# Where the product of gate and value is done, who makes the low parts of the gate weights, and the order of the second stage

## The chip, the cores and the metric

The kernel runs on one core of a Trainium2 chip. The metric is the time of one execution in microseconds (us). Five engines work side by side, each with its own list of instructions that it takes in order: PE (TensorE, matrix products), DVE (VectorE), ACT (ScalarE), POOL (GpSimd) and SP (SyncE, which here only issues DMA transfers). PEld is PE's loading of weights.

## The reference

A linear recurrence with complex decay over 768 steps (4 batches, 8 heads, 48 values per head) gives 3072 tokens of 384 values. Two feed-forward layers follow:

```python
for t in range(S):
    new_re = ar * S_re - ai * S_im
    new_im = ar * S_im + ai * S_re
    S_re, S_im = (new_re + kv, new_im)
    y[:, :, t] = np.einsum('bhd,bhde->bhe', q[:, :, t], S_re)
...
xn = x / rms * rms_g
g = xn @ w_gate                       # 384 x 1536
silu = g * (1.0 / (1.0 + np.exp(-g)))
val = xn @ w_val
x = silu * val @ w_out                # 1536 x 384
...
h = x @ w_in                          # 384 x 2048
g = h * np.clip(h + 3.0, 0.0, 6.0) / 6.0
return g @ w_out                      # 2048 x 384
```

## The kernel before

**Precision.** Each matrix product of the two layers is made in PE's rounded fp32 type as three products: every factor is split into a high part (a copy in the rounded type) and a low part (the value less its high part), and `mm3` (L743 to 746) adds high by high, high by low and low by high.

**First stage.** The recurrence is cut into seven units of 32 or 64 steps (L444 to 455 are the scan's pairs of `m` and `P` on DVE; `Sst`, `X`, `T` and `LAt` are tiles of the scan, the decay and the state). `flip` (L714 to 728) ends a part of a unit: it writes 256 tokens as `xh` (ACT) and `xl` (DVE, L728). Then `steps_M` (L748) does the first product for these tokens: 12 columns of blocks j, gate and value, three parts k, three products each of 256 columns, written to a PSUM tile `pm` that two j share; there are two such tiles. One tile takes 36 products. For each, `silu` (L761) has ACT write the silu of the gate half to `sg` (L765; two tiles), DVE multiply it by the value half in PSUM (L767), and SP store it to `u_dr` in DRAM (L769). There are 72 of these, 66 of them while the scan still runs.

**The gate weights.** They come as 12 pieces of raw 64-bit words, loaded by L320. `split_weights` (L325) turns one into high and low part `wg`: DVE decodes it in three steps (L304, 306, 308) into the single tile `wdA`, ACT checks its range (L315, 316, Abs and Sign), scales by the norm's weights (L335, three instructions) and writes the high part (L336), and DVE subtracts (L363, in a helper that sends some of its calls to POOL). The tile `wdA` is free for the next piece after that.

**The order.** All of the first stage up to the last unit is issued by `emit` (L853): a string, `ORDER`, names the step whose next part is issued, for the five engines together, and the set `ON_POOL` names the steps whose helper calls go to POOL. No scheduler moves anything there. What stands late in an engine's list waits for what is ahead of it.

**Second stage.** Blocks of 512 tokens. `steps_out1` (L900) fetches `uu` from `u_dr`, three tiles ahead (L907), splits it (`uh` on ACT, L913; `ul` on DVE, L914), multiplies by `wo` into `po`, and evicts the result as `x2b`. `steps_moe2` (L942) multiplies by `wi` into `ph`, applies the gate (ACT L957, 959, DVE L958, 960), multiplies by `w2` and stores the output. The first blocks are issued by L995 and L1003 with a fixed order of DVE and POOL, the rest by a loop at the end that the scheduler orders. In between stands a check of flags (L1007 to 1027), for which DVE waits for a small transfer.

Of the kernel before, what the change touches and what calls it, by code (L numbers as in the profile page):

```python
# [26 lines left out]
BLK = 512  # L27
KZ = 0.4995
# [205 lines left out]
def attn_moe(tc, io, dbg=None):  # L234
    nc = tc.nc
# [6 lines left out]
    u_dr = dram.tile([J1, 128, NT], F32, name="u_dr")  # L242

# [3 lines left out]
    gcol = const.tile([128, KT], F32, name="gcol")  # L247
    flags = const.tile([128, 11 * NU], F32, name="flags")
# [17 lines left out]
    nc.vector.memset(biasz[:, 5:6], -TINY_BELOW)  # L266
    SGN, MA, MB, NEGHALF, EPS = (cst[:, i:i + 1] for i in range(5))
# [57 lines left out]
    def split_weights(j):  # L325
        raw = wraw.pop(j)
        A = wdA
        yield from to_f32(raw, 768, A)
        range_check(raw, 768, j, 'act')
        yield  # L330
        wg[j] = wA.tile([128, 2, KT, 2, 128], F32R, name="wg", tag=f"w{j}")
        hi, lo = wgv(j)
        A = A.bitcast(F32).rearrange("p (k w n) -> p k w n", k=KT, w=2)
        for k in range(KT):
            nc.scalar.activation(A[:, k], A[:, k], AF.Copy, scale=gcol[:, k:k + 1])  # L335
        nc.scalar.activation(hi, A, AF.Copy)  # L336
        yield
        ttx(lo, A, hi.bitcast(F32), ALU.subtract)
# [409 lines left out]
    def steps_M(u, st, h):  # L748
# [371 lines left out]
```

## Time and profile before

| | us |
|---|---|
| median of 3 runs (lowest, highest) | 1209.68 (1208.75, 1217.75) |
| profiled execution | 1209.66 |
| its span | 1207.5 |
| busy: PE, PEld | 1073.3 (89%), 930.2 (77%) |
| busy: DVE, ACT, POOL | 780.2 (65%), 561.9 (47%), 114.4 (9%) |

The span is the profiled execution from its first to its last instruction. Busy shares over the span are averages over stages that differ: up to about 110 us the weights are decoded and the scan begins, up to about 612 us scan and first product run together, up to about 640 us the last unit's product runs, and the rest is the second stage. PE's busy time is not its useful share at full speed, since products overlap in their pipeline.

### The profile page before, as it was taken

Reading aid. Unit: us, or ns where it says so; the run is one execution under the profiler, and the core shown is the slowest. Engines: PE = TensorE matmul, PEld = TensorE weight load, DVE = VectorE, ACT = ScalarE, POOL = GpSimd, SP = SyncE. Lnnn points to the kernel's source line nnn. Section 1 sums busy time; section 2 is a strip of 40 time slices with the busy share of each in tenths; the row PEclk is TensorE's granted clock in tenths of the full one; section 3 lists DMA queues with packets and bytes.
Section 4 is the critical chain, followed back from the end, with each engine's and each line's share of the span. In section 5 each row is a group of like instructions: output and inputs, shape, how many; then the busy total and the mean of one; then the engine's idle time right before and its main releaser. Section 6 shows DMA issues by size and latency. Waiting matters only on the chain.

```text
span 1207.5 us, 24626 instructions
## 1 busy us (share of the span) xinstructions
PE 1073.3 (89%) x10264; PEld 930.2 (77%) x10264; DVE 780.2 (65%) x1483; ACT 561.9 (47%) x922; POOL 114.4 (9%) x124
## 2 busy tenths in 40 slices
PE   0175699998999998999999999899999999999997
PEld 0165588888898888888988888688888888888885
DVE  4989989899788897788878788243333333333332
ACT  5568576575656754552333444243333333333332
POOL 3010010011012003011022212000000000000000
PEclk9999799999999999999989999899999999999999
DMA  8323545635535625627356544210220220100000
GB/s 333 132 51 85 162 92 155 176 98 182 146 93 166 161 73 185 170 52 218 112 177 208 175 132 75 56 37 1 70 62 1 62 69 1 61 27 1 27 1 29
DMA packets 77977, 124.27 MB, mean 103 GB/s; under 512 B 31841, under 2 KB 50402, under 8 KB 77218
## 3 DMA queue, kind: packets, MB, share of 16 engines
q1 hardware_dynamic: 77858, 122.63, 34.9%
q8 instruction: 82, 1.34, 0.5%
q14 instruction: 37, 0.30, 0.1%
HBM read 80.33 MB, written 34.60 MB: 95 GB/s over the span
## 4 chain that ended last, share of the span: by engine, by line
PE 55%; DVE 6%; DMA 3%; ACT 1%; issue 1%; SPq 0%; DVEq 0%; ACTq 0%
PE po L745 9%; PE po L746 9%; PE po L744 9%; PE ph L744 5%; PE ph L745 5%; PE ph L746 5%; PE pm L744 3%; PE pm L745 3%; PE pm L746 3%; PE psT L606 1%; DVE m L451 1%; DMA ok_dr<-okc 1%; DVE P L455 1%; PE psY L696 1%; DMA V<-in_v_dram 1%
## 5 line engine op out<-in xcount | busy, mean ns | idle before, releaser
L744 PE MATMUL pm<-xh,wg 128*128 128x256 f32 x864 | 256.7, 297 | 30.0 <-ACT sg L765 20.6
L745 PE MATMUL pm<-xl,wg 128*128 128x256 f32 x864 | 244.6, 283 | 2.5 <-DVE xl L728 2.5
L746 PE MATMUL pm<-xh,wg 128*128 128x256 f32 x864 | 243.9, 282 | 0.0
L744 PEld LDWEIGHTS pm<-xh,wg 128*128 128x128 f32 x864 | 165.7, 192 | 41.8 <-ACT sg L765 26.0
L745 PEld LDWEIGHTS pm<-xl,wg 128*128 128x128 f32 x864 | 166.0, 192 | 3.5 <-DVE xl L728 3.5
L746 PEld LDWEIGHTS pm<-xh,wg 128*128 128x128 f32 x864 | 165.9, 192 | 0.0
L958 DVE SCALAR_TENSOR_TENSOR r<-r,ph 128x512 f32<-128x512 f32 x96 | 65.8, 685 | 106.3 <-ACT r L957 106.3
L960 DVE TENSOR_TENSOR gl<-r,gh 128x512 fp32r<-128x512 f32 x96 | 68.0, 708 | 94.6 <-ACT gh L959 94.1
L957 ACT ACTIVATE r<-ph,biasz 128x512 f32<-128x512 f32 x96 | 65.8, 687 | 117.3 <-PE ph L746 117.2
L745 PE MATMUL po<-gl,w_h 128*128 128x512 f32 x288 | 114.7, 398 | 3.8 <-DVE gl L960 3.8
L746 PE MATMUL po<-gh,w_l 128*128 128x512 f32 x288 | 114.5, 398 | 0.0
L744 PE MATMUL po<-gh,w_h 128*128 128x512 f32 x288 | 114.1, 396 | 0.0
L746 PE MATMUL ph<-x2b,wi_l 128*128 128x512 f32 x288 | 113.7, 395 | 0.0
L745 PE MATMUL ph<-x2b,wi_h 128*128 128x512 f32 x288 | 113.7, 395 | 0.0
L744 PE MATMUL ph<-x2b,wi_h 128*128 128x512 f32 x288 | 113.6, 396 | 0.0
L959 ACT ACTIVATE gh<-r 128x512 fp32r<-128x512 f32 x96 | 60.6, 632 | 107.3 <-PE po L746 83.4
L914 DVE TENSOR_TENSOR ul<-uu,uh 128x512 fp32r<-128x512 f32 x72 | 51.8, 721 | 75.5 <-ACT uh L913 75.4
L913 ACT ACTIVATE uh<-uu 128x512 fp32r<-128x512 f32 x72 | 45.3, 630 | 91.3 <-PE po L746 84.3
L745 PE MATMUL po<-ul,wo 128*128 128x512 f32 x216 | 85.1, 394 | 0.6 <-DVE ul L914 0.6
L744 PE MATMUL po<-uh,wo 128*128 128x512 f32 x216 | 85.0, 394 | 0.0
L746 PE MATMUL po<-uh,wo 128*128 128x512 f32 x216 | 84.7, 392 | 0.0
L765 ACT ACTIVATE sg<-pm 128x512 f32<-128x512 f32 x72 | 42.6, 597 | 76.4 <-PE pm L746 70.7
(143 smaller groups left out, 2013.0 us busy)
## 6 DMA issues: line engine op xcount, KB each, us to landing
u_dr<-sg SPq DMA_DIRECT2D x72, 256.0 KB, 3.0
uu<-u_dr SPq DMA_DIRECT2D x72, 256.0 KB, 2.7
raw<-in_wo_dram SPq DMA_DIRECT2D x28, 384.0 KB, 3.7
wraw<-in_wgv_dram SPq DMA_DIRECT2D x12, 768.0 KB, 13.8
S<-in_s_all_dram SPq DMA_DIRECT2D x24, 384.0 KB, 3.7
K<-k_dr SPq DMA_DIRECT2D x40, 224.0 KB, 4.4
LAt<-in_a_all_dram SPq DMA_DIRECT2D x5, 1536.0 KB, 6.8
JS<-Sst SPq DMA_DIRECT2D x52, 144.0 KB, 4.0
```

The source lines that it names most:

```text
L451: tt(out=m4, in0=la, in1=pj, op=ALU.mult)
L455: tt(out=pn, in0=m4[:, :, 0], in1=m4[:, :, 1], op=ALU.add)
L744: nc.tensor.matmul(ps, lhsT=wh, rhs=xh, start=first, stop=False)
L745: nc.tensor.matmul(ps, lhsT=wh, rhs=xl, start=False, stop=False)
L746: nc.tensor.matmul(ps, lhsT=wl, rhs=xh, start=False, stop=last)
L765: nc.scalar.activation(sg, pm[:, :, 0], AF.Silu)
L913: nc.scalar.activation(uh, uu, AF.Copy)
L914: (nc.gpsimd if n < 0 else nc.vector).tensor_tensor(out=ul, in0=uu, in1=uh.bitcast(F32), op=ALU.subtract)
L957: nc.scalar.activation(r, ph, AF.Relu, bias=biasz[:, 2:3], scale=sixth)
L958: stt(out=r, in0=r, scalar=1.0, in1=ph, op0=ALU.min, op1=ALU.mult)
L959: nc.scalar.activation(gh, r, AF.Copy)
L960: tt(out=gl, in0=r, in1=gh.bitcast(F32), op=ALU.subtract)
```

## The change

1. The second stage takes the blocks of tokens in the order 4, 5, 0, 1, 2, 3.
2. For the tokens of blocks 0 to 3 (two thirds), `silu` no longer multiplies. ACT writes the silu to `sg`, and copies the value half from PSUM to `va`; both are stored, to `u_dr` and to a new `v_dr`. `sg` and `va` share three tiles. The second stage fetches both (`uu`, `vv`) and DVE multiplies them there, ahead of the split. 48 of the 72 products move; 24 stay where they were.
3. The low part of a gate weight is made by PE: ACT scales by the negated norm weights (so `wdA` holds the negative), writes the high part with scale -1, PE adds the two by fp32 products with the identity into a PSUM tile `pw` (of the same two tiles as `pm`), and ACT evicts it with scale -1. DVE's 12 subtractions go.
4. `ORDER` and `ON_POOL` are new; the latter has 20 entries in place of 25. ACT loads its tables 37 times in place of 43.

```diff
+BLOCKS = [4, 5, 0, 1, 2, 3]
...
-    "0F1f003b7zgjbXkH000G0H0I0J0K0L120M0N0O0R0P0Q0R0R01020R0R0R020S0S0S030S03040S05060908070b0S0a0b0c0c0d0d0e0e0f0f0T0T0T0T0g0g0h0h0i0T0i0k0k0l0l0m0m0T0j0U0U0U0U0j0n"
+    "0F1f7zgj00kH3bbX000G0H0I0K0L0M120J0N0O0R0P0Q0R0R0R010R020R020S0S0S0R030S030S04050S0809060T070a0T0S0T0b0b0T0c0c0d0d0T0e0e0f0T0f0g0g0h0h0i0i0k0j0k0U0T0l0U0l0U0U0m"
...
-ON_POOL = {124, 258, 285, 376, 549, 551, 561, 656, 779, 799, 808, 827, 829, 831, 841, 936, 1103, 1107, 1109, 1111, 1113, 1125, 1356, 1360, 1372}
+ON_POOL = {2, 19, 258, 267, 493, 771, 799, 818, 819, 821, 845, 936, 1059, 1088, 1098, 1101, 1103, 1331, 1353, 1362}
...
+    v_dr = dram.tile([J1, 128, NT], F32, name="v_dr")
...
+    ngcol = const.tile([128, KT], F32, name="ngcol")
...
+    nc.vector.tensor_scalar(out=ngcol, in0=gcol, scalar1=-1.0, scalar2=None, op0=ALU.mult)
...
         for k in range(KT):
-            nc.scalar.activation(A[:, k], A[:, k], AF.Copy, scale=gcol[:, k:k + 1])
-        nc.scalar.activation(hi, A, AF.Copy)
+            nc.scalar.activation(A[:, k], A[:, k], AF.Copy, scale=ngcol[:, k:k + 1])
+        nc.scalar.activation(hi, A, AF.Copy, scale=-1.0)
         yield
-        ttx(lo, A, hi.bitcast(F32), ALU.subtract)
+
+        pw = psM.tile([128, 2, 2, 256], F32, name="pw", tag="m", bufs=2)
+        for o, n in ((0, 2), (2, 1)):
+            pwo = pw[:, o // 2].rearrange("p a n -> p (a n)")[:, 0:n * 256]
+            for i, x in enumerate((A, hi.bitcast(F32))):
+                nc.tensor.matmul(pwo, lhsT=ident, rhs=x[:, o:o + n].rearrange("p k w n -> p (k w n)"), start=i == 0, stop=i == 1)
+        yield
+        nc.scalar.activation(lo.rearrange("p k w n -> p (k w n)"), pw.rearrange("p a b n -> p (a b n)")[:, 0:768], AF.Copy, scale=-1.0)
...
-            sg = mo.tile([128, 2, 256], F32, name="sg", tag="sg")
+            sg = mo.tile([128, 2, 256], F32, name="sg", tag="sg", bufs=3)
             table(None)
             nc.scalar.activation(sg, pm[:, :, 0], AF.Silu)
             yield
+            if t0 // BLK not in BLOCKS[:2]:
+                va = mo.tile([128, 2, 256], F32, name="va", tag="sg", bufs=3)
+                nc.scalar.activation(va, pm[:, :, 1], AF.Copy)
+                yield
+                nc.sync.dma_start(u_dr[j - 1:j + 1, :, t0:t0 + 256].rearrange("j p t -> p j t"), sg)
+                nc.sync.dma_start(v_dr[j - 1:j + 1, :, t0:t0 + 256].rearrange("j p t -> p j t"), va)
+                return
             tt(out=sg, in0=sg, in1=pm[:, :, 1], op=ALU.mult)
...
+        cols = slice(BLOCKS[n] * BLK, (BLOCKS[n] + 1) * BLK)
...
-            nc.sync.dma_start(uu, u_dr[j, :, n * BLK:(n + 1) * BLK])
+            nc.sync.dma_start(uu, u_dr[j, :, cols])
+            if n >= 2:
+                hold["v", j] = mu.tile([128, BLK], F32, name="vv", tag="vv", bufs=3)
+                nc.sync.dma_start(hold["v", j], v_dr[j, :, cols])
...
+            if n >= 2:
+                tt(out=uu, in0=uu, in1=hold.pop(("v", j)), op=ALU.mult)
```

**The start, on DVE.** Three places show what the new order does. The first is the beginning of DVE's list, from the first decode of a gate weight (`wdA<-wraw`, three rows each) on; `T` and `LAt` are the decay's norm, `m` and `P` the scan. Before:

```order
13 L363 TENSOR_TENSOR T_153<-T_153,T_154 128x768
14 L363 TENSOR_TENSOR wg<-wdA,wg 128x768
15 L304 TENSOR_SCALAR wdA<-wraw 128x768
16 L306 SCALAR_TENSOR_TENSOR wdA<-wraw,wdA 128x768
17 L308 SCALAR_TENSOR_TENSOR wdA<-wraw,wdA 128x768
18 L404 SCALAR_TENSOR_TENSOR T_155<-T_153,T_155 128x768
19 L409 SCALAR_TENSOR_TENSOR T_154<-T_155,T_154 128x768
20 L412 SCALAR_TENSOR_TENSOR T_154<-T_154,T_153 128x768
21 L415 SCALAR_TENSOR_TENSOR LAt<-LAt,cst,T_154 128x768
22 L363 TENSOR_TENSOR LAt<-LAt,T_154 128x768
23 L451 TENSOR_TENSOR m_190<-LAt,P 128x192
24 L363 TENSOR_TENSOR wg<-wdA,wg 128x768
```

Now:

```order
14 L308 TENSOR_SCALAR wdA<-wraw 128x768
15 L310 SCALAR_TENSOR_TENSOR wdA<-wraw,wdA 128x768
16 L312 SCALAR_TENSOR_TENSOR wdA<-wraw,wdA 128x768
17 L415 SCALAR_TENSOR_TENSOR T_160<-T_158,T_160 128x768
18 L420 SCALAR_TENSOR_TENSOR T_159<-T_160,T_159 128x768
19 L423 SCALAR_TENSOR_TENSOR T_159<-T_159,T_158 128x768
20 L374 TENSOR_TENSOR LAt<-LAt,T_159 128x768
21 L426 SCALAR_TENSOR_TENSOR LAt<-LAt,cst,T_159 128x768
22 L308 TENSOR_SCALAR wdA<-wraw 128x768
23 L310 SCALAR_TENSOR_TENSOR wdA<-wraw,wdA 128x768
24 L312 SCALAR_TENSOR_TENSOR wdA<-wraw,wdA 128x768
25 L462 TENSOR_TENSOR m_209<-LAt,P 128x192
```

The subtractions `wg<-wdA,wg` are gone, and the third decode stands ahead of the scan's first row, where it stood behind it. In their place PE's list, which began with transposes of the scan, begins with rows for each weight; the first four are:

```order
1 L347 MATMUL pw<-wdA,ident 128x512
2 L347 MATMUL pw<-wg,ident 128x512
3 L347 MATMUL pw<-wdA,ident 128x256
4 L347 MATMUL pw<-wg,ident 128x256
5 L347 MATMUL pw<-wdA,ident 128x512
```

The fifth row is the next weight's: its decode into `wdA` waits until row 3 has read the tile.

**The silu, in the stage where scan and product run together.** DVE's list before, near the middle:

```order
637 L767 TENSOR_TENSOR sg<-sg,pm 128x512
638 L363 TENSOR_TENSOR X_104<-X_104 128x8x48
639 L482 TENSOR_REDUCE flags<-X_104 128x1
640 L767 TENSOR_TENSOR sg<-sg,pm 128x512
641 L363 TENSOR_TENSOR P<-S_4244,P 128x16x2x48
```

ACT's list now:

```order
300 L776 ACTIVATE sg<-pm 128x512
301 L780 ACTIVATE va<-pm 128x512
302 L776 ACTIVATE sg<-pm 128x512
303 L780 ACTIVATE va<-pm 128x512
304 L715 ACTIVATE Yt,flags<-psY 128x384
```

and SP's, which had one such store for each silu:

```order
94 L782 DMA u_dr<-sg 128x2x256
95 L783 DMA v_dr<-va 128x2x256
96 L635 DMA JS<-Sst 48x768
97 L636 DMA JS<-Sst 48x768
98 L782 DMA u_dr<-sg 128x2x256
```

The multiplication stood between the scan's rows on DVE; now the copy follows the silu on ACT at once, and two stores stand where one stood.

**The second stage, on DVE.** Of the first blocks before:

```order
1142 L308 SCALAR_TENSOR_TENSOR words<-raw,words 128x384
1143 L318 TENSOR_REDUCE wmin<-raw 128x1
1144 L958 SCALAR_TENSOR_TENSOR r<-r,ph 128x512
1145 L960 TENSOR_TENSOR gl<-r,gh 128x512
1146 L304 TENSOR_SCALAR words<-raw 128x384
```

and now, at about the same place:

```order
1138 L982 SCALAR_TENSOR_TENSOR r<-r,ph 128x512
1139 L934 TENSOR_TENSOR uu<-uu,vv 128x512
1140 L984 TENSOR_TENSOR gl<-r,gh 128x512
1141 L982 SCALAR_TENSOR_TENSOR r<-r,ph 128x512
1142 L984 TENSOR_TENSOR gl<-r,gh 128x512
```

The new rows `uu<-uu,vv` stand between the two halves of the gate (`r`, `gl`), ahead of the split of the block that follows.

## Rows read from the trace of the kernel before

**Rows 1.** Windows: stretch, length, busy PE, PEld, DVE, ACT, POOL; clock, DMA share, GB/s.

```profile
0.00:110.00 110.00, 33.92 (x658) 28.59 (x658) 85.62 (x173) 70.04 (x125) 15.08 (x19) 1.00 0.48 162
110.00:612.00 502.00, 457.06 (x7017) 426.15 (x7017) 427.25 (x884) 287.05 (x467) 65.54 (x74) 0.98 0.49 139
612.00:750.00 138.00, 137.16 (x685) 115.98 (x686) 111.90 (x198) 56.91 (x99) 33.73 (x32) 0.98 0.53 157
770.00:1207.00 437.00, 428.94 (x1849) 346.83 (x1847) 150.03 (x221) 143.94 (x227) 0.00 (x0) 0.99 0.11 34
```

**Rows 2.** Chain of waits that ended last, 397 to 612 us, shares by line.

```profile
by line: PE pm L744 14.0%; PE pm L746 11.3%; PE pm L745 11.3%; PE psT L606 5.9%; DVE m L451 5.3%; issue 4.1%; DVE P L455 3.9%; PE psY L696 3.6%; DMA V<-in_v_dram 3.5%; PE psU L676 3.2%; PE psS L659 3.1%; ACT sg L765 2.8%; DMA JS<-Sst 2.7%; 
```

**Rows 3.** DVE's groups: line, operation, out<-in, shapes, count | busy us, mean ns.

```profile
L767 DVE TENSOR_TENSOR sg<-sg,pm 128x512 f32<-128x512 f32 x72 | 48.8, 681 | 29.4 <-ACT sg L765 16.8 <-issue 6.3 <-PE pm L746 3.8
...
L363 DVE TENSOR_TENSOR Sst<-Sst,Tr 112x768 f32<-112x768 f32 x18 | 17.1, 948 | 5.6 <-DMA JS<-Sst 5.6
...
L363 DVE TENSOR_TENSOR wg<-wdA,wg 128x768 fp32r<-128x768 f32 x12 | 11.5, 956 | 9.0 <-ACT wg L336 8.9
...
L363 DVE TENSOR_TENSOR P<-S,P 128x768 f32<-128x768 f32 x10 | 10.6, 1074 | 0.0
...
L363 DVE TENSOR_TENSOR X<-S,P 128x1536 f32<-128x1536 f32 x5 | 8.8, 1753 | 0.1
```

**Rows 4.** Waits: engine, line, what it waited for: us in total, times, longest.

```profile
PE pm L744 <- ACT sg L765: 20.6, 25, 2.5
...
ACT L765 <- DMA u_dr<-sg: 14.2, 5, 4.2
...
PE pm L744 <- DVE sg L767: 5.2, 8, 1.9
```

**Rows 5.** Timeline of the second weight, DVE and then ACT: start, us, what.

```profile
18.01 0.56 DVE L304 TENSOR_SCALAR wdA<-wraw 128x768 int32<-128x768 int32 x1
18.61 0.96 DVE L306 SCALAR_TENSOR_TENSOR wdA<-wraw,wdA 128x768 int32<-128x768 int32 x1
19.60 0.96 DVE L308 SCALAR_TENSOR_TENSOR wdA<-wraw,wdA 128x768 int32<-128x768 int32 x1
...
21.08 0.88 ACT L315 ACTIVATE wraw<-wraw 128x768 f32<-128x768 f32 x1
21.99 0.97 ACT L316 ACTIVATE wraw<-wraw,biasz 128x768 f32<-128x768 f32 x1
...
23.78 1.29 ACT L335 ACTIVATE wdA<-wdA,gcol 128x256 f32<-128x256 f32 x3
25.11 0.84 ACT L336 ACTIVATE wg<-wdA 128x768 fp32r<-128x768 f32 x1
```

**Rows 6.** Line L561, fp32 product with the identity: two instructions, then all (min/median/max ns).

```profile
46.87 0.66 PE L561 MATMUL psF<-ident,Q 128*48 128x128 f32 x2
...
218.75 0.42 PE L561 MATMUL psF<-ident,Q 128*48 128x128 f32 x2
...
L561 PE MATMUL psF<-ident,Q x14: 272/310/449, 46.9 to 530.9; 128*48 128x128 f32 x14
```

**Rows 7.** Timeline of PE, four places.

```profile
108.91 0.58 PE L744 MATMUL pm<-xh,wg 128*128 128x256 f32 x1 [3.63 <-ACT xh L726]
...
113.01 0.28 PE L744 MATMUL pm<-xh,wg 128*128 128x256 f32 x1
113.13 0.28 PE L745 MATMUL pm<-xl,wg 128*128 128x256 f32 x1
...
762.58 0.79 PE L745 MATMUL po<-gl,w_h 128*128 128x512 f32 x1 [3.76 <-DVE gl L960]
```

**Rows 8.** The page's groups: the silu, and the weight loads of the first product.

```profile
L744 PEld LDWEIGHTS pm<-xh,wg 128*128 128x128 f32 x864 | 165.7, 192 | 41.8 <-ACT sg L765 26.0
...
L765 ACT ACTIVATE sg<-pm 128x512 f32<-128x512 f32 x72 | 42.6, 597 | 76.4 <-PE pm L746 70.7
```

**Rows 9.** The page's DMA issues: KB each, median us from issue to landing.

```profile
u_dr<-sg SPq DMA_DIRECT2D x72, 256.0 KB, 3.0
```

More of the change, by code (lines that the diff above doesn't have):

```diff
@@ new lines @@
+    "0m0n0n0j0U0o0o0p0U0p0q0q0r0j0r0s1f0t0u0V110U0t0V0t0V0y0z0V0A0v0A0V0B0V0v0w0D0C0x0W170V0E170W161g0W0W1111111h0W131118140W16181h0X2r0X2s152t151i2u0W190X1i2v0X191a"
+    "1j2w2x1b0X2F1k2y2z0X2z1b2z2z1d0X0Y1d2A0Y2A1c2A0Y1c1e0Y2A1a1n1e1l0Y2K2C0Y2K2B2C2K1m1z1o0Z2D2D0Z0Y1z2H2D0Z2G2H2D0Z2H2G1A1A1p2E0Z1B2J1B1C1C1D2K0Z1p1D1E4m1E1F1F0+2L"
+    "2L0+0Z2L2I0+2I2L0+2I1G1G1H1H2M1I1I2P0+1J2N1J2N1K1K2S1L0+2P1L4l2P2N1M2N2O1M1N1N0-0+2Q2Q1O2Q4D1O1q1P4E4F0-4G1q4H4I1P4J1r4K4L1P4M4N1s1y4O0-4Q1w4R4S1t4T0-4U1v4V4W27"
@@ new lines @@
+    "4X1u1x4Y4Z4+280-4-1Q1Q1R1R1S1S1T1T1U4P1U1V4P4P511V501W1W521X531X541Z1Y551Z285657581+1Y595a50501+295b5d0-1-1Y1-2g2b2a2Z0-2+2Z20202c2d5c5e2+212e2V5d5d215f222V225g"
+    "235h232e5i2W2424253b5j2W5k2f262R5l265m2h2-265n2i105o2-5p2j5r5s5t2k5u2k5v5q5w2l5q5q5x2R2X2n2m5y2X5z2o2R5A5B2R5D5C2R3c2R302R4p2Y4p5E305F3d2Y5G5H5D5D314p2T105I3d2U"
+    "5J4t4t313210333e104n4t324o3e4p33344q3f4r103g354s4t34103h353i3j3v3k4v4u4v3a39104v5K3a3v395L4v38363w384w3w3x364w3x3y3y3z4w3z373A3A375M4w5N5O4y4x3B3B3C4z3C3D4z3D3E"
@@ new lines @@
+    "5Q3l4z5R4B3E3F5R5P4z4y5Q5Q5R4A3F4C3G3G3H5S3H3I5S5T3I3J3J3K3l3K5S5Z5U5+5-5U6061625U3L633m6465663L3m67683L5U6a6b6c3n6d6e3u6f3o5V435V3s693r6969445V6g6h6i6j3p6k6m5V"
+    "6l3q3t4C6n6o3M5W6p3M6q3N6r6m6m3N445X5X457e6s5X8K6t3O6u476v4c6w466x6z6y8J3O6A3P6B6z6C3P483Q5X6D6E6z6F3Q6G3R6H5Y3R6I3S6J3S6K6M3T3T7i3V3U7l3V3W3U7i6L7l6N3W3X7h6M6M"
+    "3X7m3Y7h3Y6O3Z7m6P3Z3+6Q3+6R3-7b3-3U7c407z406S416T7c496U7b426V4a6W6X427c6Y6+7b6-4a427d4e4b707d717d7273744f756Z4d7n6Z6Z7n764g774g787a798-4h90914i4j7j7d7a4k927A93"
@@ new lines @@
+    "7d947d957d7a8N7o7B7j967o978N7k9b7k988N997p7f8R7B7g7p7q8R7r8R9a9c7q9d7r9e7C9f9b9b7s7C7v8L7v7D7s7w8N8M7t7w7E8O7t9g7u7H7y7u7y8P7F7I8R7x8Q9h9i7J7G8S7x9j9k7T7J9l7T9m"
+    "7U9n7U8T9p9q9r7V8T9s9t9u7V7W9v7W9w7K9x9y9o7X9z9o9A9o7K7X8T9C9D9E9B7L9F9G7M7S9H9I7P9J7Q9K9B9L9B7N9M9O9N8T9P7R7O9Q9R7Y8U7Y7Z7Z8U7+7+9O9O7-7-8U8W8080819S818U8W9T9U"
+    "9V828V9W829X839Y839Z9-848X8485858X8686888Z8+878889898a8Xad8a8b9+8X8+ada0a19-9-ada28b8Ya38ca48cae8dae8dagafaea58ea68eaga7a8a9agaaacab87alamacacanagaoapaq8far878f"
@@ new lines @@
+    "8has8hatau8i8i8jav8jaw8gay8kah8k8gah8g8l8l8raz8mahaA8m8naB8saCaDaE8n8saxaFaGaxax8oaH8oaIaKaJ8xbXaL8paM8taN8qaOaPaQaR8y8AaKaS8qaT8uahaUaVaXaKaW8yaYai8CaZ8vbB8qa+"
+    "a-b0bBbB8wb18Db2aXb38zaXb4b58Eb6b78Eaj8Fb8aj8BbC8Gb8bG8Hajd5b9bGbBajbBbYba8IbFbBbbd6bcbBbzbFbZb8akbdbzbebfbgbzbhd9bAbZbibDd9bjbkbEddbmbnbobpbAbqbrb+bsbAbtb+bud9"
+    "bvbwbxb-bKddbHbybKbHc0d7ddbybybJblbIbJd8d9c3bIdnbLdabMbLbMdbc1c4bNdddcbNbOc2c5bRblblbRbOdodpdfbQbSbQdfbSdqdrdfbTbPcfbTcfbPcgdecgchbVchdfbUbVbUdscidtciducjdvcjck"
@@ new lines @@
+    "bWckclc5cldgcmdgcmcncncocodwdxcpbWdycpdgdAcqdBcqcrdidgdhdCcrcsdDcsdEc6eBdieBdjdjc6cteBctc7dldFdjdGc8dHdIcedJdjccdKdzcudmdkc9dzdzeCcucbcaeDeEeCcddmcveCdLdNdOdPdM"
+    "eEdQdRdMdMdSeEdTdUeEdVcvdWdXdZdYeFeFcwdZdZcwcxcxd+cyeFd-cyczeFe0e1e2eGe3cze4cAe5cAcBcBeHcCcveHf+cCcDcDcFhte6cFcPe7eHe8e9hucEebecedcQeeefeaegcQeheaeaeieHejekelen"
+    "eIcRemeoepeqereseneneteuevewexcTeycYeAezcSeJeKeAeAeLcGeMcGeNcUcHeOcHcIg5cIcJg1g5cJcKePg1cKeQcLeRcLeScMeTcMeVgjeUcEeWcNeXeVeVeYcOeZe+e-cOf0f1f2c+cEf3f4cVcOf5f7cW"
@@ new lines @@
+    "f8f9c-facWfbd0fcf6fdd0f6fecXf6fXfYfXd1fffYd3fgfhd2fjfifYfkfXflfmfjfjcZfnfofpd4gkfqfrfsftfuglfwfvfxfyfwfwfzfAfBfCfDglf-fEfFg0fGfHfIfKfLfMgmfNfOgmfPfZfZfZg2fZg2hv"
+    "fZfZfZg3hwhxg6g3hxg6fQfRg8hxg7g8hxg7fSfTfUgnfVhyg4gofJg4hzgpfJfJg9fWgrgshAhLhBhMhNhOhBhPgqhQgthRfWfWhSgDhThBhUhVhXhWg9hYhBhZhXhXh+h-hDi0i1hDi2gti3i4hDi5i6gagugb"
+    "gugDhCgEgEgbgFgvi7i9iaibgwgCici8gxidiegAi8ifi8iggzgagyihhDiiijilikimgFingGgBiogGipgHiqgHililgIirgIisgJitgJiugKivgKiwgLiyixiziAiyiyiBiCiDiEiFhEhEgchEgggLgMhEgciG"
@@ new lines @@
+    "ggiHiIhFgMgNgfgNiLgdgOgOgfhHgPgdhHgPgQgQgRgihJgRgShHgegigSgUiJgegUiKgViMhHgTiNiOgViPhIgWiQgWiRgXiLiLiSgXgTghghiZgYgYiTiZgZiUgZiViZiWg+iYiXg+j0hGiYiYj0i+hGi+i-i+"
+    "j5j0j6j7gTg-j8g-j9h1jaj0hKh0hbhcj1j1hchKj1h0jbjcjdhdjejfh0jgjijjjkjljmjhjnjhjojhjpj1jqhejrjsh1juh2jtj2hkjvh2h3jwh3jxh4jyh4jzh5jujujAh5jBh6jCh6h7jDh7jEh8jFh8jHh9"
+    "jGkHkthfhakujIktjJkujKjHjHjLjMj3j3kmhhhihgkjhaj3jNlljOkjhmjPj3kjlkjQjRjSj4hijTjVhjjUjWjUjUjXhljYjZj+j-hak0k1hnkkhokvkkhok2kvhpk3k4k6k7hrhqklk5hskIkkk8k9klkaklkb"
@@ new lines @@
+    "klkcklkdklkJk5k5kekfkgklkikhlslClDlokJkwknkslskolElolFlGlHlslIkKlJkwlKkslLkKlolMkrkLkqkikikrlmkMkqq6kNkplnkplNkPlPlokQkOlQlRlSlplTlUkSlVkRlOlWlqlOlOlslXlrlYlZl-"
+    "kxlulultlul+m0kxkylukGkylvkGl-lvl-kzkSlvkTkAlvkzm1kAm2kTm3kUlwm4kUkVm5kVm6m7kWm8kWm9kXmakXmcmbkYkYkZmdkZmek-kDk-l0kCk+l0l1lyk+lykDl1kCl2l2l3kBlAlyl3kEl4kBl4lymf"
+    "kEmgmcmhl5mimcmjlzl5l6kFl6l7mkkFmll8mmmnmTmompl8mqmrmTmsmtmuk+ldmTmvl8mwl9mpmxmymzmpmAlemBlamDlfmElamCmFmGlfmHlbmQmSlgmQmQlhlilxmTq4lxocmIlcmJmRljocmUmRocmUocmR"
@@ new lines @@
+    "q5ococlBmUocmCmUoilBmCmKoiq4mVojogq4oeojq4mWogofq4mWq4q5odq4orohq5mWq5ohmLoqmWmMmNmPmOmXq7mYq5mZq8mPq5oaq5obmPoaq6obm+m-oan0obn1oyn2n3n4oun5n6oun8n7n9ounanboync"
+    "ndneoynfngnhn8ninjnlq7n8nkq7osnlq7nlotounmnnnonpovq7q7nqq6nrq7qansq6ntnuq6q6nvnyq9nwq6nxq8nznAnynBnyq8nCnDoAnEnFoAnGnHoAnInJnLnKq8nMnLnNnOnLq9nPnQq8nRq9qbnSnTq9"
+    "nUq9nVnWnYqcnXnZnYn+n-o0nYo1o2o3o4o5o6o7o9owoyokoxokolozoloAonomq8o8q9oBq8o9onoBomq9o9qaopoBqaooopqboBoooIoJoKoCoLqaoMqaqaoEqbqdqboEqbqbqaqepWoGoEqboNoOqcpWoPoE"
@@ L68 @@
+    "pWoQoRoSoFqcoTqdoUoVqcoWqcoXqcoYqdqfoZqdo+pZo-p0p1pZp2qdqdp3p5p4pZoDoUpYoDqcoUp6pZp7p8p9qdp5oHp5qfoHp+p+qfqfqfqfpXp+paqepbqfpXpcp+pdpXpepfp-qepgpiqephpjqeqepkpi"
+    "plpiqepmpnpopppqprq0pvq0q0psptpuq0pwpxpvpypvq1pzpApBpCpDpEpFpGpIpHpJpKpIpLpMpIpNpOpPpQpRpSpVpTpUpVq3q2q3q2pVq3q2"
 )
-ON_POOL = {124, 258, 285, 376, 549, 551, 561, 656, 779, 799, 808, 827, 829, 831, 841, 936, 1103, 1107, 1109, 1111, 1113, 1125, 1356, 1360, 1372}
+ON_POOL = {2, 19, 258, 267, 493, 771, 799, 818, 819, 821, 845, 936, 1059, 1088, 1098, 1101, 1103, 1331, 1353, 1362}
@@ L975, in evict @@
                 nc.scalar.activation(ob, hold["ps"][:, m], AF.Copy)
-            nc.sync.dma_start(io["out"][m * 128:(m + 1) * 128, n * BLK:(n + 1) * BLK], ob)
+            nc.sync.dma_start(io["out"][m * 128:(m + 1) * 128, BLOCKS[n] * BLK:(BLOCKS[n] + 1) * BLK], ob)
         LAG = 2
```

32 lines of the change are left out of this document (removed).

## The prediction

> **What bounds the kernel now.** I read the windows by stage first, then the chain of waits, then VectorE's (DVE's) groups, the waits, and the timeline of the start. The windows [rows 1] show four stages. Up to 110 us PE is busy 33.9 us and DVE 85.6: weights are decoded and the scan starts. From 110 to 612, where scan and first product run together, PE is busy 457.1 of 502 us and DVE 427.3, with ScalarE (ACT) at 287.1. From 612 to 750 PE is busy 137.2 of 138 and DVE 111.9. From 770 on PE is busy 428.9 of 437 and DVE 150.0, a third. So DVE's work can cost time only before 612. There neither engine alone sets the pace: the chain of waits from 397 to 612 [rows 2] goes through PE's first product for 14.0 + 11.3 + 11.3% and through further PE lines for 15.8%, together 52%; two DVE lines of the scan follow with 5.3 and 3.9%.
>
> **The change part by part.** The sum is made against the profiled execution, 1209.66 us (span 1207.5 and 2.2 around it), which is the median of the runs to 0.02 us.
>
> *Product of gate and value.* 48 of the 72 products of the silu with the value leave DVE in the middle stage, at 681 ns [rows 3]: 32.7 us. In their place ACT copies the value half out of PSUM 48 times; no such copy is in the trace, the nearest row is the silu on the same shape, 597 ns [rows 8], so 28.7 us on an engine with 215 us idle there [rows 1]. It is bounded below by nothing, if it falls wholly into idle time, and above by all 28.7 on the chain; I take nothing, since ACT holds 2.8% of that chain [rows 2]. PE waited 5.2 us for the product on DVE to free a PSUM tile, and 20.6 us for the silu [rows 4]; the first goes, the second stays, with the copy behind it. SP gets 48 more stores; a store of this size lands after 3.0 us [rows 9], and DMA engines are busy half of the stage [rows 1].
>
> *Low parts of the gate weights.* 12 subtractions of 956 ns [rows 3] leave DVE, nine of them before the first product. PE does 4 fp32 products with the identity for each weight, and ACT 12 more evictions.
>
> *New order, other choice of POOL.* Counting the order, between DVE and POOL: 6 more Sst at 0.948, 3 more P at 1.074, 2 fewer X of 1536 columns at 1.753 [rows 3], and of four other forms five leave DVE and three come to it, at about 0.95. That is 5.7 + 3.2 - 3.5 - 1.9 = +3.5 us on DVE.
>
> *Middle stage.* DVE: -32.7 - 2.9 (three subtractions) + 3.5 = -32.1, from 427.3 to 395.2. If PE is the bound, nothing is gained; if DVE sets the pace, 502 x 395.2 / 427.3 = 464, a gain of 38. I take a half of 32.1, because PE holds about half of the chain, and 5 for PE's waits on the product: **-21**. The ends 0 and -38 stay for the range.
>
> *Start.* Every weight goes through one tile, wdA, so its turns follow one another. A turn now: decode 0.56 + 0.96 + 0.96, Abs and Sign 0.88 + 0.97, scale 1.29, high part 0.84 [rows 5], subtraction 0.96 [rows 3], about 7.5 us. In the changed kernel the last 0.96 is replaced by three PE products of 512, 512 and 256 columns (the fourth doesn't read wdA), ten times 128 columns. An fp32 product with the identity of 128 columns is in the trace as two records: 0.66 us together early, 0.42 at 218.8, with one record 0.45 at most and 0.27 at least [rows 6]. So a record follows the other by some 0.24 us early and 0.15 later, and the ten cost 4.8 or 3.0 us. The turn becomes about 10.7 or 8.9 us with ACT's pauses. The granted clock reads 1.00 over the whole start [rows 1], so the level is read from durations: early ones are those of the 1.2 GHz level, later ones of the 2.4 GHz level. Counting the order, 11 decodes instead of 9 stand ahead of the flip that completes the first product's input, though DVE's own work up to there falls from 86 to 76 us. From the second decode at 18.0 [rows 5] nine turns end at 114 or 98; with what stands between in the order (each instruction begins when its engine's last one and its inputs are done), I get 121 or 109 for the first product, which began at 108.9 [rows 7]. Cost 0 to +12; I take **+7**, nearer to the 1.2 GHz end, because PE is busy only a third of the start and has nothing else between two turns.
>
> Here the Trainium skill, "TensorE: Matmul & The Clock Gate", section "HAM oscillation", speaks: PE left waiting goes back to its low level and pays the start again at each return. The trace agrees in one place: after 3.76 us idle the product at 762.58 took 0.79 us [rows 7]. By that rule all twelve turns run at the low level, +12, and the total would be about 1201.
>
> *Second stage.* 48 products (both inputs in SBUF; nearest row 681 ns, 32.7 us), 48 fetches (nearest row 3.0 us to landing [rows 9]). DVE is idle two thirds of the time from 770 on [rows 1], the values are fetched three tiles ahead: **0**. If that cover were gone the 32.7 us would be paid. About ten of the products fall into the tighter stretch 612 to 750, 6.6 us on a DVE with 26 idle. The new block order begins with tokens whose products are long stored. The pause at 762 stays as it is.
>
> Sum: 1209.7 - 21 + 7 + 0 = **1196**, 1.2% less. With the other ends of the start and a middle of -14 to -24, the likeliest case itself holds 1186 to 1204.
>
> **The rivals.**
>
> *DVE sets the pace of the middle.* For it: 85% busy over the stage with a scan whose steps wait for one another; against: PE's 52% of the chain. Then -38 and a start of +7, or of +2 with PE warm: 1174 to 1180, 1178 taken.
>
> *PE is the bound of the middle.* For it: 457 of 502 busy, so at most 45 us are there to gain, and of PE's waits the largest, 20.6 us, ends with the silu and stays. A gain of 0 to 10 and a start of +7 to +12: 1206 to 1218, 1210 taken. [...]
>
> *Slower: the ring of store tiles.* sg and va now share three tiles, two taken per silu, where two tiles took one each. The second silu after one needs a tile whose store has landed: 0.6 + 0.6 + issue + 3.0 us. One PSUM tile is 36 products at 0.12 us [rows 7], 4.3 us, so silus in close succession wait on ACT, and PE behind it on the PSUM tile. Already now ACT waited 14.2 us in five such places, 2.8 each [rows 4]. It decides if about half of the 48 come that close: 24 x 2.8 = 67 us, half of it reaching the end, +34: 1209.7 + 7 - 21 + 34 = 1230 (1222 to 1235). Against it: 66 silus in 502 us are 7.6 us apart on average.
>
> **How the numbers follow.** Likeliest case 0.42 (1186 to 1204), DVE's pace 0.17 (1170 to 1186), PE's bound 0.24 (1203 to 1218), store ring 0.17. Range: 1174 to 1219 leaves out the ring and the edge of DVE's case. One per cent, 12 us, is what a measurement here tells from no change: below 1197.6 lie two thirds of the likeliest case and all of DVE's, 0.27 + 0.17 = 0.44; within, the rest of the likeliest and PE's, 0.39; above 1221.8 the ring, 0.17.
>
> **What would show it.** The first product begins at 113 to 121 if the start is right; products of the identity 0.24 us apart there. From first product to last silu the stage takes about 480 us; 500 means that PE is the bound, 465 that DVE was. ACT's wait for u_dr or v_dr stores over 40 us means the ring. In the second stage PE's share stays at 98%, with no wait on the new product. The forecast is wrong if first product and middle both stay where they are, or if PE waits for the value's copy longer than the 5 us it waited for the product.

## The result and the profile after

The changed kernel took 1223.69 us (median of 20 runs, 1214.15 to 1227.57), the kernel before 1213.54 in runs beside it (20 runs, 1207.46 to 1221.65). The ratio is 1.0077, 95% interval 1.0056 to 1.0098: **0.8% slower**, where 1.2% faster was forecast. The profiled execution took 1219.19 us, span 1217.4; like that of before it lies 4 us under its median, so the two traces compare evenly. Between the same marks (the starts of the first product's first record, of DVE's last `xl` and of the last silu) they read:

| stretch | before, us | after, us | difference |
|---|---|---|---|
| start to first product | 108.9 | 115.4 | +6.5 |
| first product to last flip (the middle) | 502.9 | 507.2 | +4.3 |
| last flip to last silu | 28.5 | 25.7 | -2.8 |
| second stage | 567.2 | 569.1 | +1.9 |

The same four stretches in the windows of the changed kernel (columns as in [rows 1]; the last cut lies 0.2 us behind the start of the last silu):

```profile
0.00:115.40 115.40, 64.68 (x737) 38.52 (x737) 76.88 (x161) 79.76 (x140) 19.31 (x21) 0.81 0.43 147
115.40:622.60 507.20, 468.55 (x7032) 433.15 (x7032) 399.84 (x841) 303.75 (x505) 59.91 (x66) 0.98 0.56 164
622.60:648.50 25.90, 25.89 (x218) 25.71 (x219) 19.91 (x35) 8.12 (x16) 7.75 (x8) 1.00 0.72 219
648.50:1217.00 568.50, 554.57 (x2376) 447.24 (x2374) 277.10 (x442) 196.29 (x317) 27.45 (x25) 0.99 0.25 77
```

and the middle before, between its own marks:

```profile
108.90:611.80 502.90, 457.69 (x7018) 426.49 (x7018) 428.15 (x885) 288.15 (x467) 65.34 (x74) 0.98 0.49 138
```

DVE's work in the middle did fall, from 428 to 400 us, but the stage didn't shorten: what DVE doesn't work it now waits, 107 of 507 us where it was 75 of 503. PE is idle there for 38.7 us in place of 45.2, so it does wait less, but it is busy for 468.6 us in place of 457.7. Of these 10.9 us more, 8.2 are the low-part products of the two gate weights that come in this stretch (the window of the tile `pw`: PE, PEld, ACT):

```profile
115.40:622.60 507.20, 8.18 (x16) 3.97 (x16) 1.60 (x2) 0.98 0.56 164
```

The chain of waits from 397 to 622 shows PE with more of it than in [rows 2], the first product now 19.7 + 15.8 + 15.7%, and the silu on ACT 5.1 for 2.8%:

```profile
by line: PE pm L755 19.7%; PE pm L757 15.8%; PE pm L756 15.7%; PE psT L617 7.1%; ACT sg L776 5.1%; PE psY L707 5.1%; PE psS L670 3.5%; PE psY L698 2.8%; DMA JS<-Sst 2.7%; PE psU L687 2.4%; DVE X L374 1.7%; issue 1.6%; PE psX L732 1.4%; DVE 
```

Its waits, against [rows 4]: PE's wait for the silu is about as long as before, its 5.2 us for the product are gone, with one wait of 4.3 us for the value's copy in their place, and ACT's copy waits for stores:

```profile
PE pw L347 <- ACT wdA L339: 37.2, 6, 15.8
...
PE pm L755 <- ACT sg L776: 22.4, 32, 0.7
...
PE pm L755 <- ACT va L780: 4.3, 1, 4.3
...
ACT va L780 <- DMA u_dr<-sg: 12.7, 9, 2.9
```

The start on PE's timeline. From start to next start, the three products that hold `wdA` take 1.87 + 1.71 + 0.79 us, and the next turn begins 10.9 us after the first:

```profile
15.80 2.08 PE L347 MATMUL pw<-wdA,ident 128*128 128x512 f32 x2 [15.80 <-ACT wdA L339]
17.67 1.91 PE L347 MATMUL pw<-wg,ident 128*128 128x512 f32 x2
19.38 0.96 PE L347 MATMUL pw<-wdA,ident 128*128 128x256 f32 x2
20.17 0.60 PE L347 MATMUL pw<-wg,ident 128*128 128x256 f32 x2
26.68 2.08 PE L347 MATMUL pw<-wdA,ident 128*128 128x512 f32 x2 [5.92 <-ACT wdA L339]
```

And the moved product and the copy, in DVE's and ACT's groups, 704 ns and 595 ns:

```profile
L934 DVE TENSOR_TENSOR uu<-uu,vv 128x512 f32<-128x512 f32 x48 | 33.8, 704 | 44.5 <-DMA uu<-u_dr 35.9 <-issue 3.5 <-DMA out_dram<-ob 2.6
```

```profile
L780 ACT ACTIVATE va<-pm 128x512 f32<-128x512 f32 x48 | 28.6, 595 | 19.2 <-DMA u_dr<-sg 12.7 <-PE pm L757 6.2 <-ACT Yt L723 0.3
```

### The profile page after: what moved, and what is told of

Read it like the earlier page. It is cut to its first block, busy times and chain, and to the rows that moved or that the text cites. A ratio compares the mean times of both kernels' runs of the same rounds, so it can differ in the third digit from the quotient of the medians.

```text
span 1217.4 us, 25010 instructions
## 1 busy us (share of the span) xinstructions
PE 1113.7 (91%) x10360; PEld 944.6 (78%) x10360; DVE 773.7 (64%) x1477; ACT 587.9 (48%) x976; POOL 114.4 (9%) x119
## 4 chain that ended last, share of the span: by engine, by line
PE 73%; DVE 12%; ACT 7%; DMA 5%; issue 2%; SPq 0%; POOL 0%; DVEq 0%; ACTq 0%; POOLq 0%
PE po L756 9%; PE po L757 8%; PE po L755 8%; PE pm L755 8%; PE pm L756 6%; PE pm L757 6%; PE ph L755 5%; PE ph L756 5%; PE ph L757 5%; PE pw L347 4%; PE psT L617 3%; PE psY L707 2%; ACT sg L776 2%; PE psS L670 1%; PE psU L687 1%
```

## The experiments

All against runs of before on the same chip. "Middle" is from the first product to the last flip in the one profiled execution; differences of some 5 us between two such single values say nothing.

| kernel | median us | ratio to before (95%) | first product at | middle |
|---|---|---|---|---|
| before | 1213.5 | 1 | 108.9 | 502.9 |
| changed | 1223.7 | 1.0077 (1.0056, 1.0098) | 115.4 | 507.2 |
| 1 before, 48 DVE products out | 1204.6 | 0.9949 (0.9928, 0.9969) | 108.6 | 499.8 |
| 2 before, 288 PE products out | 1210.5 | 0.9980 (0.9952, 1.0007) | 108.5 | 506.7 |
| 3 before, product moved | 1252.4 | 1.0331 (1.0288, 1.0374) | 108.7 | 546.5 |
| 4 new order, old parts | 1229.5 | 1.0151 (1.0121, 1.0180) | 115.4 | 521.8 |
| 5 before, cuts 1 and 2 | 1196.5 | 0.9885 (0.9836, 0.9935) | 108.6 | 487.4 |
| 6 changed, cut 2 | 1211.3 | 0.9993 (0.9959, 1.0027) | 116.0 | 497.6 |
| 7 changed, low parts on DVE | 1224.8 | 1.0104 (1.0064, 1.0144) | 115.4 | 516.8 |
| 8 before, product moved, ring of 5 | 1213.7 | 1.0010 (0.9980, 1.0040) | 108.7 | 508.2 |
| 9 changed, ring of 5 | 1216.9 | 1.0029 (1.0003, 1.0055) | 118.0 | 506.5 |
| 10 changed, two decodes later | 1225.0 | 1.0099 (1.0068, 1.0130) | 111.9 | 513.9 |
| 11 changed, PE's products unused | 1227.0 | 1.0117 (1.0090, 1.0144) | 119.4 | 511.4 |
| 12 changed, product on DVE | 1226.7 | 1.0101 (1.0070, 1.0132) | 118.9 | 517.7 |
| 13 before, new list | 1243.5 | 1.0250 (1.0211, 1.0289) | 114.6 | 532.3 |
| 14 before, old list then new | 1241.4 | 1.0231 (1.0187, 1.0275) | 108.9 | 544.6 |
| 15 before, new list then old | 1222.8 | 1.0075 (1.0049, 1.0101) | 114.6 | 512.3 |
| 16 before, idle products on PE | 1233.7 | 1.0161 (1.0125, 1.0196) | 124.5 | 515.6 |
| 17 before, ring of 5 | 1207.4 | 0.9951 (0.9926, 0.9976) | 108.7 | 502.9 |

**Does DVE's load, or PE's, set the middle? (1, 2, 5, 6)**

Experiment 1 leaves the 48 products out:

```diff
-            tt(out=sg, in0=sg, in1=pm[:, :, 1], op=ALU.mult)
+            if t0 // BLK > 3:
+                tt(out=sg, in0=sg, in1=pm[:, :, 1], op=ALU.mult)
```

> The kernel before, with the 48 DVE products of blocks 0 to 3 left out altogether (silu alone is stored; no copy on ACT, no second store, nothing in the second stage). It takes 48 x 0.681 = 32.7 us off DVE and nothing else. Theory A (PE and its waits on the silu hold the middle stage, DVE's load doesn't): first product to last flip stays at 503 us, within 8, and the time within 8 us of before. Theory B (DVE's load sets the middle, and copy, stores or new order ate the gain): 16 to 38 us faster.

Experiment 2 leaves out the third product for the last k (`mm3` gets a last argument that says whether it is made):

```diff
-            mm3(hold[j // 2][:, j % 2, w], wh[:, k, w], wl[:, k, w], xh[:, k], xl[:, k], k == 0, k == KT - 1)
+            mm3(hold[j // 2][:, j % 2, w], wh[:, k, w], wl[:, k, w], xh[:, k], xl[:, k], k == 0, k == KT - 1, k < KT - 1)
```

> The kernel before, with the third product (low weight by high token) of the last of the three k left out in the first product: 288 products of 256 columns at 0.118 us, 34 us off PE, about as much as the first experiment takes off DVE; 31 us of it lies ahead of the last flip. Theory A: 20 to 34 us faster. Theory B: at most 10 us faster, most of it after the last flip, where PE alone works.

Both at once, and the second in the changed kernel:

> The kernel before with both cuts of the first two experiments: 48 DVE products left out (32.7 us off DVE) and 288 of PE's products (34 us off PE). Alone they gave 6.2 and 2.5 us. Theory C (PE and DVE are both near their limit in the middle and wait for each other in turn, so that one alone can't shorten it): much more than the sum, 20 to 35 us faster than before. Theory D (the middle is held by the order in which steps stand in the lists, by ACT or by transfers, and by neither load): about the sum, 6 to 12 us faster.

> The changed kernel with the same 34 us off PE. Theory C: DVE has been relieved there already (399 of 506 us), so PE is the bound and the cut counts: 15 to 30 us faster than the changed kernel, 1190 to 1206. Theory D: at most 8 us faster.

The windows of the middle of 1, 2 and 5, in this order:

```profile
108.60:608.40 499.80, 460.42 (x7018) 429.83 (x7018) 403.12 (x837) 287.89 (x467) 66.75 (x74) 0.98 0.50 140
```

```profile
108.50:615.20 506.70, 447.97 (x6754) 413.38 (x6754) 428.27 (x885) 289.03 (x469) 66.98 (x74) 0.94 0.49 137
```

```profile
108.60:596.00 487.40, 433.13 (x6754) 400.94 (x6754) 404.43 (x838) 288.26 (x469) 68.60 (x74) 0.97 0.51 143
```

Experiment 1 took 25 us of DVE's busy time out of the middle and the time fell by 6 us, 0.5%: less than theory B wanted, within A's 8. Experiment 2 took 264 products out of the middle, 31 us at the high level; the time fell by 0.2%, not clear of none, so A's 20 to 34 fell too. Both cuts gave 1.15%, 14 us, more than 6.2 + 2.5, less than C's 20, and with an interval that reaches both; the profiled middle shortened by 15.5 us where the single cuts changed it by -3.1 and +3.8. That leans to C. In the changed kernel the same cut of PE gave 0.8% (0.9993 against 1.0077), 10 us: PE counts more once DVE is relieved, but not the 15 that C asked for.

Part of what the second experiment didn't gain went into PE's clock: granted 0.94 in that middle, where before had 0.98 [rows 1]. The products that were left ran slower: 31 us of products were taken out, and PE's busy time in the middle fell by 9.7 us, from 457.7 to 448.0. Over the 96 runs of before that stand beside the experiments the time falls by 8.1 us for each 0.01 of granted clock (correlation -0.94). The median clock of experiment 2 is 0.970 and of the runs of before beside it 0.983; if that slope is taken for the effect of the clock, this is some 11 us, an estimate. So experiment 2 doesn't bound what 31 us less of PE's work would be worth at an unchanged clock.

**What did moving the product cost? (3, 8, 9, 17)**

> The kernel before with only the product moved (copy on ACT in the place of the DVE product, two stores, ring of three, block order 4, 5, 0 to 3, products in the second stage), under the old order and with the low parts on DVE. Theory A: within 6 us of before, perhaps 5 faster for PE's waits on the product. Theory B with copy and stores as the cause: within 6 or up to 10 slower, while the first experiment is 16 or more faster. Theory B with the new order as the cause: 16 to 38 faster.

```diff
-                va = mo.tile([128, 2, 256], F32, name="va", tag="sg", bufs=3)
+                va = mo.tile([128, 2, 256], F32, name="va", tag="sg", bufs=5)
```

(the same for `sg`)

> The third experiment (product moved, old order, 40 us slower than before, ACT's copy waiting 52.8 us for stores) with five tiles in place of three for sg and va. If the ring of store tiles was the cause (the rival of the prediction, met under the old order), ACT's wait for stores falls below 15 us and 20 to 40 us come back: 1212 to 1232. If the copy itself on ACT was the cause, under 10 us come back.

> The changed kernel with five tiles in place of three for sg and va. There ACT's copy waited 12.7 us for stores in nine places (52.8 us in the product moved under the old order, where five tiles brought back 39 us). If the ring still costs the changed kernel its gain, 8 to 15 us come back, to 1209 to 1216; if the new order had already spread the silus so that the ring costs little, 0 to 5 us.

ACT's copy under the old order with three tiles, and then with five:

```profile
ACT va L774 <- DMA u_dr<-sg: 52.8, 14, 7.6
```

```profile
ACT va L774 <- DMA u_dr<-sg: 3.0, 2, 2.6
```

The ring was the whole of it: 3.3% slower with three tiles, level with five. So under the old order the move, freed of the ring, gains nothing over before, though it takes as much off DVE as experiment 1. In the changed kernel the copy waits less for stores, 12.7 us for 52.8, and five tiles still bring back 0.5% (1.0029 against 1.0077). And the kernel before had such waits too [rows 4]:

> The kernel before with five tiles in place of two for sg, nothing else. There ACT waited 14.2 us in five places for a store before it could write the next silu. If these waits are on the path that sets the middle, as three of five tiles were in the product moved under the old order, 4 to 12 us faster than before, which would beat both kernels; if ACT has slack there, within 3 us.

It is 0.5% faster than before (1207.4 us), the only version here that leaves nothing out and beats both kernels. ACT no longer waits for stores in its trace, but the profiled middle is as long as before, 502.9 us, so these single profiles don't show where the gain lies. With a ring of five on both sides (8 against 17: 1.0010 against 0.9951) the move under the old order costs 0.6%.

**What do order and low parts do? (4, 7, 12, 10, 11, 16)**

Experiment 4 is the changed kernel with the old parts: the products and the low parts again on DVE, at the places in the list where ACT's copy and PE's products stood.

> The changed kernel with the product back on DVE in the first stage and the low parts back on DVE: the new order and choice of POOL alone (with ring of three and the new block order). Theory A: within 6 us of before. Theory B with the new order as the cause: 10 to 30 us slower than before. If the start's +6.5 us comes from the low parts on PE, the first product begins at 108 to 111.

> The changed kernel with the low parts of the gate weights back on DVE, at the place where PE's products stand. If the low parts on PE cost the start its +6.5 us, the first product begins at about 109 here; if the new order did (it began at 115.4 with the new order alone), it stays at 114 to 116. In the middle three subtractions come back, 2.9 us: 0 to 5 us either way.

> The changed kernel with the product back on DVE in the first stage for all tokens, at the places of ACT's copy; low parts stay on PE. With the new order alone 1229, with the product moved in it 1225, with both moved 1224. If the parts add up, the moved product is worth 5 us in the middle and this comes to 1226 to 1230; if DVE's load mattered now that the order is made for the move, 1232 or more; if not at all, 1222 to 1225.

The order, with the new choice of POOL, ring and blocks that come with it, costs 1.5% with the old parts. Its middle:

```profile
115.40:637.20 521.80, 479.10 (x7017) 445.86 (x7017) 425.48 (x891) 278.39 (x455) 58.60 (x66) 0.95 0.47 135
```

PE is idle there no longer than before, 42.7 us for 45.2, but it is busy 479.1 us where it was busy 457.7 with as many records, at a granted clock of 0.95 for 0.98. So the loss in the middle shows as slower products and not as a longer sum of PE's waits; in 7 and 13 PE's busy time is 478 and 482 us, at 0.95 and 0.94. By what the order brings the clock down isn't shown.

Under the order the moved product brings 0.5% (7) and the low parts 0.5% (12), each at the edge of what the intervals tell, and both together 0.7%, clear of noise. So the parts do gain under it, and the order takes twice as much. The first product begins at 115.4 with the low parts on DVE too, so most of the start's loss is the order's; with PE's products it came at 115.4 to 119.4 in five profiles, 117.5 in the mean, so they may add some 2 us.

> The changed kernel with the tenth and eleventh gate weight's steps moved behind the flip that completes the first product's input, as far as the old order had them. If these two decodes (5 us on DVE, with their ACT work) are what the new order's start costs, the first product begins at 107 to 111 in place of 115.4; the time falls by as much only if the product doesn't then wait for the two weights: 1217 to 1224. If the start is held by something else, the first product stays at 114 to 116.

Half of it is the two decodes, 111.9 in place of 115.4, and it is given back at once: the next stretch, to the eighth flip, is 111.7 us for 104.6. One weight more has its products on PE in that stretch, and the stretch's first record takes 0.58 us, as in 7 below.

Experiment 11 keeps PE's products and makes the low parts on DVE (the scales of `wdA` and of the high part get their old sign back):

```diff
+        nc.vector.tensor_tensor(out=lo, in0=A, in1=hi.bitcast(F32), op=ALU.subtract)
...
-        nc.scalar.activation(lo.rearrange("p k w n -> p (k w n)"), pw.rearrange("p a b n -> p (a b n)")[:, 0:768], AF.Copy, scale=-1.0)
```

> The changed kernel with the low parts made by DVE as before, while PE's products with the identity stay and nobody reads them (ACT's eviction goes). With the products away altogether (low parts on DVE) the first 110 us of the middle took 6 us longer and more first products ran at PE's low level: 208 records against 161. If the low parts' move gained through PE's clock, this kernel keeps 160 to 180 such records and a stretch of 104 to 107 us from the fourth to the eighth flip; if it gained through DVE's relief, 200 or more and 109 to 112.

The stretch from the fourth to the eighth flip, in the changed kernel, in 7 and in 11; the granted clock is the third number from the end:

```profile
115.40:219.90 104.50, 94.44 (x1234) 83.54 (x1234) 92.75 (x197) 74.17 (x118) 4.52 (x8) 0.92 0.57 168
```

```profile
115.40:226.10 110.70, 98.52 (x1218) 90.23 (x1218) 94.50 (x199) 72.93 (x116) 5.73 (x8) 0.85 0.54 161
```

```profile
119.40:224.10 104.70, 94.75 (x1234) 84.18 (x1234) 94.52 (x200) 72.91 (x116) 4.53 (x9) 0.90 0.55 165
```

The stretch is short where PE's products stand ahead of it, read or not (102.7 to 105.7 us in the changed kernel and in 6, 9, 11 and 12), and long without them (110.7 in 7, 110.8 in 4); 7 and 11 have the same work on DVE in it, 94.5 us. What the low parts' move gains within this stretch, 6 us, is PE's clock: in its first 5 us PE runs 40 records in the changed kernel and 23 in 7. With the products PE was busy for 65 of the 115 us ahead of the first product, without them for 33; the first record takes 0.39 us with them and 0.58 without, the two rows being

```profile
115.36 0.39 PE L755 MATMUL pm<-xh,wg 128*128 128x256 f32 x1 [0.79 <-ACT xh L737]
```

```profile
115.38 0.58 PE L750 MATMUL pm<-xh,wg 128*128 128x256 f32 x1 [0.42 <-ACT xh L732]
```

The Trainium skill's "TensorE: Matmul & The Clock Gate", section "HAM oscillation", says that a PE which is left waiting falls back to its low level and begins its next work there. The trace agrees, with 0.58 us for the first record of 7, and here the added products were what kept PE awake.

Over the whole kernel less is left of it. In 11 and 12 the first product began some 4 us later, so that the eighth flip comes at 224.1 and 224.5 us, 2 us ahead of 7 and 4 (226.1 and 226.2), and 11 as a whole is no faster than 7 (1.0117 and 1.0104).

> The kernel before, with four fp32 products with the identity added on PE for each of the first ten gate weights (of the high part alone, so that the decode tile is not held; nobody reads them). They do no work but keep PE busy in the start, as the low parts do in the changed kernel. If that was how the low parts' move gained (7 us in the first stretch of the middle), the first products begin at the high level (0.39 us or less in place of 0.58) and before becomes 3 to 8 us faster; if the gain needs the new order, within 3 us. If the products stand in the way of the scan on PE, 3 to 8 slower.

That gain did not carry over: in the old list such products stand in the way, PE waited at them for 21.8 us on ACT's high part and 13.9 us on a DVE product, and before became 1.6% slower.

**Where does the order lose? (13 to 15)**

> The kernel before with nothing but the new list of the order: same parts, same blocks, ring of two, and the old choice of POOL. The new order with the new choice of POOL came to about 16 us over before. If the list is the cause: 10 to 22 us slower than before; if the choice of POOL was: within 5.

> The kernel before with the old list up to the flip that completes the second 256 tokens (214 us) and the new list from there on. If the new order loses its time early (first product at 115 in place of 109, first stretch of the middle 111 in place of 105): within 5 us of before. If it loses it all along the middle: 6 to 12 slower.

> The kernel before with the new list up to the flip that completes the second 256 tokens and the old list from there on, the counterpart. Loss early: 10 to 16 us slower than before; loss all along: 5 to 10 slower.

The list loses on its own, 2.5%; 4, which has the new choice of POOL, ring and blocks beside it, stands 1.0% better. New then old costs 0.75%: +5.1 us up to the fourth flip (114.6 for 109.5) and +11.5 from there to the eighth (116.1 for 104.6, at a granted clock of 0.82 for 0.92), after which it runs like before (396.2 and 397.7 us). Old then new costs 2.3%, some of it at the join (the stretch after it is 105 us for 85). So the list loses early and later; both expectations that named one place fell. Which of its rows do it isn't settled.

## Why the prediction was wrong

- **Middle, the step that failed.** "I take a half of 32.1, because PE holds about half of the chain, and 5 for PE's waits on the product: -21." It measured +4.3, which single profiles don't tell from 0. DVE's work fell by 28 us, near the 32.1, but taking the products out altogether gives -3 in the profiled middle and -6 in the medians (1), and moving them gives nothing (8). A share of the chain is not a rate at which an engine's work turns into time: the relieved engine waited for the others instead, and PE's idle time, which is all that such a relief can take away, fell by 6.6 us. The sum also had no term for PE's own new work in the middle, the 8.2 us of low-part products.
- **The order as a count.** The new order was entered as +3.5 us of DVE's work. Run with the old parts it costs 1.5% (4), which the traces show as products that run slower (PE busy 479 us in the middle for 458). An order sets when each engine works and when it stands, and that has no price in a sum of durations. This is the largest term that was missing.
- **Start.** +7 was taken and +6.5 came, by luck, for a wrong reason. The turns of `wdA` come near what was worked out (4.4 us on PE for 4.8, turns of about 10.4 for 10.7), though the terms listed for a turn add up to 11.3 and not 10.7: PE's first product starts at 36.43 us, ahead of the high part at 36.81, which the sum puts in front of it. Nor do all twelve turns run at the low level: from start to next start the first product of the first six took 1.87 us, that of the one at 79.30 us took 0.99. But the first product begins about as late without these turns (4, 7). Five kernels with PE's products and this list in the start gave 115.4 to 119.4, so the term is known to some 4 us.
- **The low level as a cost only.** The text priced the low level of the products; that they lift the clock of the stretch behind them, worth 6 us in it, was not seen.
- **Second stage.** Forecast 0, came +1.9, which single profiles don't tell from 0. 704 ns for 681, and PE's pause is 4.27 us for 3.76.
- **Copy on ACT.** 595 ns for 597; taking nothing for it held only where a tile of the ring was free when it was due.
- **The rivals.** "PE is the bound" was closest: no gain in the middle, 1206 to 1218. By its own terms, no gain and +12, it reaches 1221.7. But PE alone isn't shown to be the bound either (2). "DVE sets the pace" fell (1). The ring of store tiles is a true mechanism, priced at 34 us and worth 39 under the old order; in the changed kernel it costs 0.5%.
- **Bounds and signs.** The likeliest case with a middle of -14 and a start of +12 comes to 1207.7, not 1204. The stage of "about 480 us" ends at the last flip, not at the last silu, which before stood 531 us behind the first product. Neither sign of being wrong came: the first product moved, and PE waited 4.3 us for the copy where 5 was the mark. They were no test of the middle alone.
- The Trainium skill's "Perfetto Trace Analysis", section "Identifying the Most-Contended Engine", says that the engine with the highest occupancy is the most contended one, with TensorE's headroom judged by the share of its peak rate and by its weight loads, and to improve that engine first. By loads PE (426 us) and DVE (428 us busy) stand level in the middle. They gave 0.5 and 0.2% when each was relieved of over 30 us, and 1.15% together, so here the measurement names neither as the one.

## What to carry to other kernels

Where two engines are both near full and issue in order, price a relief of one by an experiment that simply leaves the work out, before building anything: it bounds the gain at the cost of one edit, as long as nothing else moves with it, as PE's clock did in experiment 2. A hand-made or planned order belongs to the parts it was made for; measure it alone, since a change of parts and order together hides which of them pays, and look at the granted clock and at an engine's busy time as well as at its waits. Count the tiles of a ring by how many one step takes, not by how many there are: a ring that stores drain is a wait of one landing each time two steps come close.

## What the hardware showed

- Time goes with PE's granted clock from run to run of the same kernel: 1202.8 us at 0.992, 1219.3 at 0.972, 8.1 us for each 0.01 over 96 runs.
- Work taken off PE can lower its clock: with 31 us less of it in the middle the granted clock there went from 0.98 to 0.94, and the median over whole runs from 0.983 to 0.970.
- The successor of an fp32 product of 512 columns with the identity started 1.87 us after it at a granted clock of 0.50 (at 26.68 us in the changed kernel), and 0.86 us after it at 1.00 (at 134.08).
